# K and Q of the later units read in pieces of two tokens, transposed in two halves by VectorE, in a new order of steps

## The chip, the core and the metric

The kernel runs on one core of one Trainium2 chip. The core has TensorE (matrix products, "PE" in the profile, with its weight loads "PEld"), VectorE ("DVE"), ScalarE ("ACT"), GpSimd ("POOL") and SyncE ("SP"), which run beside each other and meet by semaphores, and 16 DMA engines between HBM and on-chip memory. The metric is the time of one execution in microseconds.

## The reference

A layer of linear attention with the delta rule, and on its output a mixer with a low-rank token product and a two-layer channel network. Batch 4, 8 heads, 768 tokens, 48 values a head, all in 32-bit floats; the mixer has 384 channels, 1536 hidden ones and rank 32.

```python
k_n = k / (np.linalg.norm(k, axis=-1, keepdims=True) + 1e-06)
for t in range(S):
    y[:, :, t] = np.einsum('bhd,bhde->bhe', q[:, :, t], state)
    v_old = np.einsum('bhde,bhd->bhe', state, kt)
    state = state + bt[:, :, :, None] * np.einsum('bhd,bhe->bhde', kt, vt - v_old)
...
x = attn_out.transpose(0, 2, 1, 3).reshape(B, S, H * D)
h = x.transpose(0, 2, 1) @ U @ V
u = x + h.transpose(0, 2, 1)
out = u + np.maximum(u @ w_ch1, 0.0) @ w_ch2
```

## The kernel before

**Units and chunks.** A batch element has two units (`NU = 2`) of 384 tokens; a unit is all 8 heads over 6 chunks (`UC`) of 64 tokens (`L`). There are 8 units `n`; unit `n` lives in `slots[n % 2]`, 9792 floats on each of 128 partitions, in which `views` cuts overlapping places: `kn` and `qn` (K and Q, tokens on partitions), `kq` (K and Q transposed, values on partitions), `pg` and `qk` (products K K' and Q K'), `diag` (the 32x32 diagonal blocks of K K', which share their place with `qk`), `vn` (V).

**A unit's work.** `load` (L311) fetches K, Q and V, on the queue of SP for heads 0 to 3 and of GpSimd for heads 4 to 7 (K of unit 0 partly on ScalarE's). `grams` (L407) brings K and Q into `kq` and forms their products (`products`, L444, matmuls L451); ScalarE copies the diagonal blocks into `diag` (L456 and L460 from unit 3 on, L463 with VectorE's L466 before) and the whole product into `pg` (L470); VectorE masks the products with Q (L478). `blocks` (L491) transposes the diagonal blocks into `gs` (L511), inverts them by substitution on VectorE (L520, L522), transposes back (L526, L533), and joins the blocks to chunks on TensorE (L581 to L634, with copies L643 and memsets L647). `recur` (L655) then walks the chunks in order: prediction from the state (L729, or L753 in the first two units), its difference from V (L735, L760), correction (L742, copied by L745), state update (L770, added by L776), and the outputs (L677, L684), copied to `X` by L667.

**How K and Q reach `kq`.** In units 0 and 1 TensorE transposes them (L231). From unit 2 on (`n >= NU`), K is loaded a second time, as `kb`, and Q only so, in blocks of 32 tokens: partitions are the 32 tokens, one block after another lies along the row, values 0 to 31 on one quarter of the partitions and 32 to 47 on the next (L331 to L335). `turn_blocks` (L433) waits for them and lets VectorE transpose 32x32 blocks straight into `kq`, one instruction of 768 elements a partition for each pair `j` of head groups (L440). K's blocks lie in the place of `pg`, Q's in that of `qn`.

**The mixer.** `front` (L979, L1105, L1108) does the token product, `wide` the channels: first product L1182 with ReLU L1152, second product L1270 added to `X` by L1216 and stored by L1225; L1007 is the first product of the first tokens, done ahead. Six columns of the hidden layer are summed cross-wise (L1203, L1210), so that seven products of half size do for eight. The last batch element uses another scheme of products (L960, L945, L930, L941). Some steps exist in two forms: on the whole 128x128 array, or cut into four 64x64 parts (`crossed`, L219) so that they share a tiling with the recurrence; a "q" in the order chooses the second.

**What sets the order.** The parts are generators; each yields before every step the engine it is for, and `run` (L191 on) resumes them in the sequence of `ORDER`, a list of some 2,700 numbers, each the number of a part, with a bank of the accumulators after a dot. So `ORDER` is the program order of all engines and of both DMA queues at once. `need` makes a part wait until others have emitted a key; it only orders the program, and semaphores between the engines follow from what each instruction reads and writes.

Of the kernel before, what the change touches and what calls it, by code (L numbers as in the profile page):

```python
# [14 lines left out]
L = 64  # L15
BK = 32
# [7 lines left out]
def kernel(ctx: ExitStack, tc: tile.TileContext, q: bass.AP, k: bass.AP, v: bass.AP, beta: bass.AP, moe_U: bass.AP, moe_V: bass.AP, moe_w_ch1: bass.AP, moe_w_ch2: bass.AP, out: bass.AP):  # L24
    nc = tc.nc
# [9 lines left out]
    UC = NC // 2  # L35
# [47 lines left out]
    295 71 295 294 71 61 294 61 294 61 71 297 179.1 294 61 75 300 298 295.2 68 71 295 298 301q 295 294 300  # L83
# [6 lines left out]
    162 330 311 9 329 328 328 328 328 328 329.1 333 329 331 325.0 329 9.2 334q 329 9 334 9.1 325 334 9 9.2  # L90
    334 9 325 334 345.1 9.2 346 9 9.2 345 335q 9 345 61 345 9.2 335 9 347.1 325 9.2 335 335 9 348.0 335 9.2
    347 349 9 9.2 347 336q 9 330 330 336 347 348 9.2 89 89 89 89 205 205 205 205 205 205 205 205 90 90 90 90
# [3 lines left out]
    362 341q 359 362 359 362 341 359 359 85 360.2 357 341 341 357 352 78 357 78 78 9.0 341 78 9 9.1 360 364  # L96
    9 360 363 360 9.0 78 365.1 78 85 9 9.2 342q 9 85 85 85 85 9.0 78 342 9 85 85 365 85 366.2 342 9.0 85 365
# [3 lines left out]
    371 107 85 106 85 344 180 107 106 106 85 107 85 85 180.2 85 372 180 181.0 85 372 97 92 373q 333 350 87  # L101
# [6 lines left out]
    387 102 102 102 383 391 407 391 407 10 102 102 406.1 10.0 102 182q.2 10 102 408 10.0 102 408 182 409 102  # L108
    102 102 409 10 102 102 102 10.2 420 406 405.0 10 406 102 10.2 410q 102 10 102 405 410 406 102 405 421.2
    102 10.1 410 410 10 10.0 410 10 422.1 102 421 423 10.0 102 10 102 421 10.0 421 411q 10 10.2 422 411 10  # L110
# [153 lines left out]

    def blocked(n, i):
        return slots[n % 2][:, 7680:9216] if i else slots[n % 2][:, 4608:6144]

    def in_blocks(n, i):
        return blocked(n, i).rearrange('p (j g x t) -> p j g x t', j=2, g=2, t=BK)
    units = [views(slots[n % 2]) for n in range(N)]  # L270
# [1087 lines left out]
```

## Time and profile before

| | |
|---|---|
| Median of 3 runs | 582.97 us (580.89 to 583.97) |
| Profiled execution | 582.44 us |
| Its span, first to last instruction | 580.0 us |
| Mean granted TensorE clock | 0.976 |
| TensorE, VectorE, ScalarE, GpSimd busy | 538.4, 406.9, 239.7, 134.0 us |
| DMA | 89194 packets, 35.12 MB |

Busy times are from the profiled execution. An engine that is busy little can still be waited for; the chain that ended last follows from the last instruction back to what released each step. A line of the groups reads: line, engine, operation, what it writes and reads, shapes, count, then total busy us and mean ns, then idle time of that engine just before and what ended it.

### The profile page before, as it was taken

The numbers are of one execution on the slowest core, as the hardware profiler recorded it, in microseconds if no ns is written. First come the engines' busy times: TensorE is split into PE (matmuls) and PEld (weight loads), VectorE is DVE, ScalarE is ACT, GpSimd is POOL, SyncE is SP. The second block draws the span as 40 slices with busy tenths as digits, with TensorE's granted clock in tenths as the row PEclk, the third lists the DMA queues.
The fourth block names the chain that finished last, engine by engine and source line by source line (L and its number), as shares of the span: only waits on it lengthen the run. The fifth ranks groups of instructions, "written<-read, shape, count | busy, mean of one in ns | idle before, by whom it ended". The sixth has DMA issues, their size and how long they took to land.

```text
span 580.0 us, 24828 instructions
## 1 busy us (share of the span) xinstructions
PE 538.4 (93%) x11061; PEld 449.4 (77%) x11061; DVE 406.9 (70%) x1010; ACT 239.7 (41%) x523; POOL 134.0 (23%) x229
## 2 busy tenths in 40 slices
PE   5666788999999999999999999999999999999997
PEld 4555676669779778789879877989889769656997
DVE  5799776899969346999978789987713344656532
ACT  3786775442423545146144532632343330346000
POOL 8141341642200470723018207400010000000000
PEclk9998669999989999999999999999999999999999
DMA  9977654450300252530133223220000100000001
GB/s 144 185 191 189 166 147 97 73 102 16 88 13 2 45 114 29 105 78 19 33 44 75 60 39 73 45 62 3 17 2 3 45 2 1 27 0 1 28 15 41
DMA packets 89194, 35.12 MB, mean 61 GB/s; under 512 B 75200, under 2 KB 86976, under 8 KB 89088
## 3 DMA queue, kind: packets, MB, share of 16 engines
q1 hardware_dynamic: 80800, 24.10, 19.9%
q0 software_dynamic: 6688, 9.15, 7.7%
q8 instruction: 86, 1.41, 1.0%
q10 hardware_dynamic: 1600, 0.30, 0.3%
q14 instruction: 20, 0.16, 0.1%
HBM read 28.80 MB, written 4.72 MB: 58 GB/s over the span
## 4 chain that ended last, share of the span: by engine, by line
PE 82%; DVE 6%; issue 4%; DMA 3%; ACT 2%; SPq 1%; POOL 0%; DVEq 0%; POOLq 0%
PE P L1270 25%; PE P L1182 15%; PE P L219 10%; PE P L960 7%; PE P L451 3%; PE P L1007 2%; PE P L742 2%; PE P L677 2%; PE P L729 2%; PE P L770 2%; PE P L684 2%; DMA slot<-in_k_dram 1%; PE P L1105 1%; PE P L979 1%; DVE xt L522 1%
## 5 line engine op out<-in xcount | busy, mean ns | idle before, releaser
L1182 PE MATMUL P<-ut,w_sb 128*128 128x256 f32 x384 | 91.0, 391 | 0.8 <-issue 0.5
L1182 PEld LDWEIGHTS P<-ut,w_sb 128*128 128x128 f32 x384 | 72.2, 193 | 12.6 <-issue 1.8
L1270 PE MATMUL P<-w_sb,hs 128*128 128x192 f32 x456 | 79.3, 329 | 0.0
L1270 PEld LDWEIGHTS P<-w_sb,hs 128*128 128x128 f32 x456 | 74.1, 190 | 1.7 <-DVE X L1216 0.7
L522 DVE TENSOR_TENSOR xt<-xt,prod 128x112 f32<-128x112 f32 (+21 forms) x200 | 64.1, 320 | 5.2
L520 DVE TENSOR_TENSOR prod<-gs,xt 128x112 f32<-128x112 f32 (+21 forms) x200 | 63.8, 319 | 4.7
L1216 DVE TENSOR_TENSOR X<-X,P 128x192 f32<-128x192 f32 x85 | 29.3, 349 | 51.1 <-PE P L1270 46.9
L1152 ACT ACTIVATE hs<-P 128x512 f32<-128x512 f32 x48 | 28.7, 597 | 73.5 <-PE P L1182 56.2
L219 PE MATMUL P<-ut,w_sb 64*64 64x256 f32 x768 | 51.2, 382 | 0.3
L667 ACT COPY X<-P 64x192 f32<-64x192 f32 x96 | 30.0, 312 | 34.8 <-PE P L684 33.7
L647 POOL MEMSET slot<- 32x384 f32 x32 | 13.7, 431 | 127.5 <-PE P L618 56.0
L1270 PE MATMUL P<-w_sb,S 128*128 128x192 f32 x240 | 41.6, 329 | 0.0
L1270 PEld LDWEIGHTS P<-w_sb,S 128*128 128x128 f32 x240 | 38.9, 190 | 0.8 <-DVE prod L520 0.6
L643 ACT COPY slot<-zz 32x384 f32<-32x384 f32 x64 | 34.4, 542 | 12.1 <-DVE zz L599 6.1
L451 PE MATMUL P<-slot 48*64 48x64 f32 x1536 | 33.4, 241 | 6.3 <-ACT slot L428 4.6
L335 POOL DMA_DIRECT2D slot<-in_k_dram x48 | 30.2, 635 | 37.5 <-issue 29.2
L451 PEld LDWEIGHTS P<-slot 48*64 48x64 f32 x1536 | 30.1, 153 | 10.1 <-ACT slot L428 5.0
L335 POOL DMA_DIRECT2D slot<-in_q_dram x48 | 29.9, 628 | 34.0 <-DVE rest L735 21.5
L776 DVE TENSOR_TENSOR s<-s,P 128x192 f32<-128x192 f32 x40 | 14.0, 350 | 32.1 <-PE P L770 25.6
L342 POOL DMA_DIRECT2D slot<-in_v_dram x32 | 21.1, 664 | 50.2 <-DVE s L776 17.0
L219 PEld LDWEIGHTS P<-ut,w_sb 64*64 64x64 f32 x768 | 25.3, 133 | 8.3 <-ACT seen L224 0.8
L1270 PE MATMUL P<-w_sb,slot 128*128 128x192 f32 x180 | 30.4, 327 | 0.9 <-DVE X L1216 0.9
(188 smaller groups left out, 1005.3 us busy)
## 6 DMA issues: line engine op xcount, KB each, us to landing
w_sb<-in_moe_w_ch_dram SPq DMA_DIRECT2D x14, 384.0 KB, 5.2
out_dram<-X SPq DMA_DIRECT2D x22, 192.0 KB, 2.0
slot<-in_k_dram SPq DMA_DIRECT2D x36, 72.0 KB, 3.9
slot<-in_k_dram POOLq DMA_DIRECT2D x32, 72.0 KB, 3.2
slot<-in_v_dram POOLq DMA_DIRECT2D x32, 72.0 KB, 3.3
slot<-in_v_dram SPq DMA_DIRECT2D x32, 72.0 KB, 3.3
X<-in_moe_w_ch_dram SPq DMA_DIRECT2D x6, 384.0 KB, 4.9
wide<-in_moe_w_ch_dram SPq DMA_DIRECT2D x4, 384.0 KB, 4.7
```

The lines of the kernel that those rows point to most:

```text
L219: nc.tensor.matmul(to[half(g)], w[half(r), half(g)], x[half(r)], start=start, stop=stop, skip_group_check=True)
L335: queue.dma_start(out=in_blocks(n, int(name == 'q'))[quarter(2 * par + y), j, g, :, 0:cols.stop - cols.start], in_=of[:, :, cols])
L451: nc.tensor.matmul(p_g[half(g ^ par * i), par, c], kq[rows, c, j, 0, half(g)], kq[rows, c, j, i, half(g)], start=True, stop=True)
L520: nc.vector.tensor_tensor(out=prod, in0=gb[:, :, j, j + 1:, None].to_broadcast([128, split, w, m]), in1=xb[:, :, j:j + 1, 0:m].to_broadcas ...
L522: nc.vector.tensor_tensor(out=xb[:, :, j + 1:, 0:m], in0=xb[:, :, j + 1:, 0:m], in1=prod, op=ALU.subtract)
L643: nc.scalar.copy(pg[quarter(i), :, at, :, a:a + BK], thirds(h)[quarter(i)].rearrange('p r (c j) t -> p r c j t', j=2))
L667: nc.scalar.copy(x[half(c % 2), c // 2, 4 * D * g:4 * D * (g + 1)].rearrange('p (j r d) -> p r j d', r=2, d=D), states(p_y)[half(g)])
L960: nc.tensor.matmul(banks[x], w1_sb[:, 4 * a[0] + e, a[1]] if isinstance(a, tuple) else w1_mixes[a][:, e], tokens(*t) if isinstance(t, tupl ...
L1152: nc.scalar.activation(hs[:, fs[0]:fs[1] + 1:fs[1] - fs[0]], p_f, ACTF.Relu)
L1182: nc.tensor.matmul(p_f[:, x], w(x, t), ut[:, t], start=t == 0, stop=t == KT - 1)
L1216: nc.vector.tensor_tensor(out=to, in0=to, in1=p, op=ALU.add)
L1270: nc.tensor.matmul(to, of[0], of[1], start=of[2], stop=of[3], skip_group_check=True)
```

## The change

K (`kb`) and Q of units 2 to 7 are read in pieces of two neighbouring tokens, 96 values that are contiguous in memory. Partition `t` gets tokens 2t and 2t+1 of each chunk: on the first quarter values 0 to 79 of the 96, on the next 32 to 95. Token 2t's values start at column 0 of a piece and token 2t+1's at column 48, so VectorE now transposes twice (`u` 0 and 1), each time 32 columns of every piece, and writes every second column of `kq`. Pieces are 80 columns wide in place of 32 columns for each token: K's occupy columns 4608 to 6527 of the slot, which reaches into `diag`, and Q's 7680 to 9599. For this the wait for both of K's transpositions moves ahead of the copies to `diag`. DMAs are as many as before. In the changed program the lines from the end of `ORDER` to L264 stand one higher in number, those from there to `turn_blocks` one lower (L335 becomes L334), L440 and L451 stay, and all later ones stand one higher (L456 becomes L457, L1182 becomes L1183).

`ORDER` is a new list throughout, of 2,694 tokens in place of 2,670; the banks and the sequence of almost all steps differ. Of it only the first line of each list is shown.

```diff
-    0 1 0 150 1 149 0 1 2 0 1 37 37 36 37 36 22 14.0 36 22 36 2 213 213 21 39 2 38 37 15.1 21 39 38 39 214.2
+    0 1 0 149 1 0 1 2 0 1 37 37 36 37 36 2 2 14.0 38 37 36 22 36 213 213 22 21 147 15.1 38 39 38 22 38 214.2
...
@@ -262,11 +263,9 @@
         diag = slot[:, 6144:6144 + BK * BK].rearrange('p (e t r) -> p e t r', t=BK, r=2)
         return (kn, kq, pg, qk, qn, vn, diag, kz)
 
-    def blocked(n, i):
-        return slots[n % 2][:, 7680:9216] if i else slots[n % 2][:, 4608:6144]
-
-    def in_blocks(n, i):
-        return blocked(n, i).rearrange('p (j g x t) -> p j g x t', j=2, g=2, t=BK)
+    def in_pairs(n, i):
+        at = (4608, 7680)[i]
+        return slots[n % 2][:, at:at + 4 * UC * (D + BK)].rearrange('p (j c g w) -> p j c g w', j=2, g=2, w=D + BK)
     units = [views(slots[n % 2]) for n in range(N)]
     nc.vector.memset(P[:, :, 0:256], 0.0)
     for i in range(2):
@@ -328,11 +327,11 @@
             if name == 'kb' or name == 'q' and n >= NU:
                 for s in range(4):
                     j, par = divmod(s, 2)
-                    of = src[b, 4 * g + s, hf * UC * L:(hf + 1) * UC * L, :].rearrange('(x t) d -> t x d', t=BK)
+                    of = src[b, 4 * g + s, hf * UC * L:(hf + 1) * UC * L, :].rearrange('(c t u) d -> t c (u d)', c=UC, u=2)
                     for y in range(2):
-                        cols = slice(BK * y, min(BK * y + BK, D))
+                        cols = slice(BK * y, (D + BK, 2 * D)[y])
                         yield op(e)
-                        queue.dma_start(out=in_blocks(n, int(name == 'q'))[quarter(2 * par + y), j, g, :, 0:cols.stop - cols.start], in_=of[:, :, cols])
+                        queue.dma_start(out=in_pairs(n, int(name == 'q'))[quarter(2 * par + y), j, :, g, 0:cols.stop - cols.start], in_=of[:, :, cols])
                     if s % 2:
                         emitted((name, n, g, j))
                 continue
@@ -435,9 +434,10 @@
             if i == 0 and j == 0:
                 yield op('pool')
                 nc.gpsimd.memset(diag[:, CS // 2:], 0.0)
-            yield op('dve')
-            of = in_blocks(n, i)[:, j].rearrange('p g (c u) t -> p c g (u t)', u=2)
-            nc.vector.transpose(kq[:, :, j, i].rearrange('p c (g t) -> p c g t', g=2), of)
+            for u in range(2):
+                yield op('dve')
+                to = kq[:, :, j, i].rearrange('p c (g t u) -> p c g u t', g=2, u=2)[:, :, :, u]
+                nc.vector.transpose(to, in_pairs(n, i)[:, j, :, :, D * u:D * u + BK])
             emitted(('turned', n, i, j))
             begin(products(j, i))
 
@@ -450,6 +450,7 @@
                     rows = half(par, D)
                     nc.tensor.matmul(p_g[half(g ^ par * i), par, c], kq[rows, c, j, 0, half(g)], kq[rows, c, j, i, half(g)], start=True, stop=True)
             if i == 0:
+                yield need(*[('turned', n, 0, y) for y in range(2) if n >= NU])
                 to = diag[:, 0:CS // 2].rearrange('p (c j) t r -> p r c j t', j=2)[:, :, :, j]
                 if n >= LIGHT:
                     yield op('act')
@@ -465,7 +466,7 @@
                         yield op('dve')
                         nc.vector.scalar_tensor_tensor(out=to[:, r], in0=p_g[:, r, :, BK:L], scalar=even[:, 1:2], in1=to[:, r], op0=ALU.mult, op1=ALU.add)
                 emitted(('diag', n, j))
-                yield need(*[('diag', n, y) for y in range(2) if n == 0], *[('turned', n, 0, y) for y in range(2) if n >= NU])
+                yield need(*[('diag', n, y) for y in range(2) if n == 0])
                 yield op('act')
                 nc.scalar.copy(pg[:, :, :, j], p_g)
                 for y in range(2) if n in SPLIT else ():
```

More of the change, by code (lines that the diff above doesn't have):

```diff
@@ L53 @@
     ORDER = """
[29 rows of a table removed]
-    295 71 295 294 71 61 294 61 294 61 71 297 179.1 294 61 75 300 298 295.2 68 71 295 298 301q 295 294 300
[6 rows of a table removed]
-    162 330 311 9 329 328 328 328 328 328 329.1 333 329 331 325.0 329 9.2 334q 329 9 334 9.1 325 334 9 9.2
-    334 9 325 334 345.1 9.2 346 9 9.2 345 335q 9 345 61 345 9.2 335 9 347.1 325 9.2 335 335 9 348.0 335 9.2
-    347 349 9 9.2 347 336q 9 330 330 336 347 348 9.2 89 89 89 89 205 205 205 205 205 205 205 205 90 90 90 90
[3 rows of a table removed]
-    362 341q 359 362 359 362 341 359 359 85 360.2 357 341 341 357 352 78 357 78 78 9.0 341 78 9 9.1 360 364
@@ L97 @@
-    9 360 363 360 9.0 78 365.1 78 85 9 9.2 342q 9 85 85 85 85 9.0 78 342 9 85 85 365 85 366.2 342 9.0 85 365
[3 rows of a table removed]
-    371 107 85 106 85 344 180 107 106 106 85 107 85 85 180.2 85 372 180 181.0 85 372 97 92 373q 333 350 87
[6 rows of a table removed]
-    387 102 102 102 383 391 407 391 407 10 102 102 406.1 10.0 102 182q.2 10 102 408 10.0 102 408 182 409 102
-    102 102 409 10 102 102 102 10.2 420 406 405.0 10 406 102 10.2 410q 102 10 102 405 410 406 102 405 421.2
-    102 10.1 410 410 10 10.0 410 10 422.1 102 421 423 10.0 102 10 102 421 10.0 421 411q 10 10.2 422 411 10
[7 rows of a table removed]
@@ L118 @@
-    112 10 441.1 112 112 10.2 112 419 10 112 112 119 443 10.2 447 441 119 447 448q 119 441 10 441 119 119
-    10.2 119 448 119 10 443 459.1 10.2 448 448 10 119 119 448 119 10.0 119 459 119 460 444.2 10 119 459 10.0
-    119 459 119 461.1 10 444 10.0 119 449 119 444 119 449 119 119 119 450 119 462 119 10 119 450 119 119 119
-    10.2 463 461 465.0 10 461 119 10.2 461 451q 119 10 464 10.1 119 451 10 10.2 451 466.1 465 10 119 10.2
-    465 451 465 119 10 119 10.0 119 451 10 119 468.2 467 10.0 10 452 119 119 119 466 119 10.0 464 452 10 119
@@ L123 @@
-    466 466 119 119 453 469 119 119 119 453 119 119 464 468 211 140 140 211 211 211 211 211 211 140 140 141
-    139 140 140 138 212 140 212 140 212 211 212 138 141 141 131 112 470 162 212 468 455q 119 468 212 119 471
-    212 183.0 471 212 141 131 141 455 119 141 119 183 141 455 471 183.1 141 119 455 139 183 139 455 132
-    183q.2 119 474 472.0 119 183 119 475.1 119 119 119 184.2 119 475 473 119 475 456 119 119 475 119 119 472
[5 rows of a table removed]
-    504.2 485.1 11 504 504 11.0 184q.2 11 485 11.0 501 492 11 184 136 136 136 492 136 136 136 494 506 507
@@ L133 @@
-    485 507 494 507 508 501 185.0 509 505.2 11.1 11 501 495q 495 185 493 11.1 510.0 495 505 495 11 505 136
-    505 136 11.1 495 136 11 136 11.2 185.1 511 136 136 496 136 11 136 512 136 136 496 136 136 136 136 513
-    497 514 136 136 136 11.2 515 510 136 515 516q 136 510 136 185 136 11 516 136 11.2 510 516 11 516 531 530
-    529 528 527.1 11.0 516 528 11 531.2 129 531 532 11.0 527 531 517q 527 11 527 517 533.2 11.0 517 517 11
-    11.1 517 11 535.0 534 11.1 533 11 518q 11.1 518 11 11.1 535 518 533 518 11 528 535 518 535 11.1 533
@@ L138 @@
-    531.0 536 531 529.2 529 530 537 519 528 528 537 528 519 520 539 520 521 540 521 523 541 529 530 530 530
-    530 523 543 542 11 542 542 537 524 522 544 529.2 545 529 524 529 529 531 531 538.1 546 11.2 525q 11 11.0
-    525 11 11.2 538 525 11 525 538 538 525 11.0 547.2 548 11 549 11.1 549 526q 11 11.0 526 11 11.1 550.0 552
-    547 11 551 11.1 547 552 553q 547 11 162 514 11.2 553 11 11.1 553 553 11 564.2 11.1 553 11 11.1 565 550
-    564 11 554q 564 564 550 554 566.1 11.2 554 550 554 11 11.0 554 11 568.2 567 11.0 566 11 555q 566 566
@@ L143 @@
-    11.0 555 11 568 555 555 568 568 555 186.1 569 570 556q 186 556 186.0 556 556 186 556 570 186.2 571 186
[11 rows of a table removed]
[30 rows of a table added]
+    295.2 295 294 68 298 301q 294 295 290 74 294 301 44 295.2 295 301 301 295 68 297 295 301 68 68 9.1 68 68
[5 rows of a table added]
+    332 311 329 9 332 61 328 328 328 328 328 328 329.0 333 329 331.2 162 331 329 9.1 334q 331 9 329 324.2
+    9.1 334 9 9.0 334 345.1 330 324 9 162 9.0 324 334 324 9 9.2 334 9 9.0 346 345 347.2 9 345 335q 345 9.0
+    335 9 9.1 335 335 9 335 348.0 9.1 349 347 9 347 9.1 347 336q 9 330 336 330 9.2 348 90 89 90 89 89 90 89
[3 rows of a table added]
@@ new lines @@
+    91 339 330 88 9.2 360 357.0 361 356 341q 357 9 361 357 9.2 357 341 357 85 9 362.0 341 9.2 356 341 356 9
+    78 78 9.1 78 341 9 361 9.2 78 363.1 78 365 9 364 9.2 78 362 342q 9 362 85 362 9.2 342 340 85 366.0 9 363
[4 rows of a table added]
+    371.0 100 180 373 100 104 374q 85 85 101 374 181.1 101 108 109 374 98 374 109 108 98 108 109 374 181
[6 rows of a table added]
+    182q.1 10 102 408 406.0 10.2 102 182 408 407 409 102 407 102 10 102 409 102 102 102 405.1 420 10.2 102
+    406 410q 102 406 10 405 102 405 10.2 406 410 102 10 421.1 102 10.0 410 410 10 102 10.2 410 10 102 10.0
@@ new lines @@
+    423 162 421 422.2 10 102 421 10.0 421 411q 10 102 10.1 102 411 10 424.0 102 10.1 411 422 411 10 422 422
[7 rows of a table added]
+    112 419 10 112 112 112 119 119 10.1 447 441 10 447 448q 443 119 443 10.1 448 119 10 459.2 119 10.1 119
+    448 119 441 448 10 441 119 119 10.1 119 448 10 459 119 444.0 461 119 119 10.1 459 119 459 449 119 10 119
+    119 119 449 119 444 444 460.2 462 10.1 119 450 119 119 119 450 119 10 119 119 10.0 119 463 465.1 460 10
+    119 10.0 460 464 451q 460 10 119 10.2 119 451 10 119 10.0 451 466.2 465 10 119 10.0 465 464 451 10 119
@@ new lines @@
+    465 10.0 119 451 10 119 468.1 467 10.0 119 466 10 119 10.0 119 452 10 119 466 119 162 452 119 119 119
+    453 469 119 119 119 453 119 162 119 468 139 141 141 211 212 212 211 212 211 211 212 212 211 141 140 140
+    212 140 212 141 211 470 162 211 212 468 455q 471 466 140 141 471 468 119 183.0 140 141 119 464 211 131
+    131 141 140 119 139 119 455 140 183 139 140 131 183.2 139 455 119 138 455 141 138 183 455 138 119 119
+    138 183q.1 119 119 132 183 184.0 132 472.2 474 471 475.1 119 472 473 119 472 456 119 119 475 119 119 475
[5 rows of a table added]
@@ new lines @@
+    11.2 503 184q.1 11 502 497 11.2 136 490 11 136 136 497 490 501 136 136 492 506 136 184 136 501 501 492
+    507 507 507 508 136 505.2 509 185.0 136 491 493q 11.1 493 11 136 136 11.1 505 493 136 493 505 11 505 136
+    136 510.1 185 11.2 493 11 136 136 11.2 185.0 511 136 512 136 185 494 136 136 136 136 136 494 136 136 513
+    129 495 136 136 136 514 11 514 11.0 515 510 11 515 516q 510 136 510 136 136 516 527.2 11.0 516 516 531
+    11 529 528 11.1 528 516 11 531.0 531 532 11.1 527 11 517q 527 531 527 517 528 533.1 11.0 517 517 11 528
@@ new lines @@
+    11.2 517 11 535.0 534 11.2 533 11 518q 533 11.2 518 11 11.2 535 518 518 11 535 535 533 518 11.2 529.0
+    536 529 531.1 531 528 529 537 519 530 528 11 530 530 519 530 530 530 520 539 531 520 521 540 531 521 523
+    541 542 542 523 537 543 537 542 524 544 529.0 545 529 522 524 529 529 538.2 546 11.1 525q 11 11.0 525 11
+    11.1 538 525 11 525 538 538 525 11.0 547.1 548 11 549 11.2 549 526q 11 11.0 526 11 547 11.2 552 550.0 11
+    551 547 11.2 547 553q 11 11.1 553 11 564.2 11.1 553 553 11 11.1 553 11 550 11.1 565 564 11 564 554q 550
@@ L155 @@
+    550 564 554 11.1 566.0 554 11 554 11.2 554 11 568.1 567 11.2 566 11 555q 566 566 11.2 555 11 568 555 555
+    568 568 555 186.0 569 570 570 556q 186 570 556 186.2 556 556 186 556 186.1 571 186 163 163 187.0 163 557
[11 rows of a table added]
     """
```

139 rows, old and new, of the table ORDER are left out of this document.

## The prediction

> **What bounds the kernel now.** I read the shares of the page first, then the slices, the chain that ended last, busy time by stretch, TensorE's waits, and the timeline where the recurrence and the mixer alternate.
>
> ```profile
> span 580.0 us, 24828 instructions
> PE 538.4 (93%) x11061; PEld 449.4 (77%) x11061; DVE 406.9 (70%) x1010; ACT 239.7 (41%) x523; POOL 134.0 (23%) x229
> PEclk9998669999989999999999999999999999999999
> PE 82%; DVE 6%; issue 4%; DMA 3%; ACT 2%; SPq 1%; POOL 0%; DVEq 0%; POOLq 0%
> ```
>
> TensorE is busy 538.4 of 580.0 us and holds 82% of the chain. The kernel can shorten only where TensorE does less or idles less; it idles 41.6 us. The stretches tell where (columns: length, then busy us and count of PE, PEld, DVE, ACT, POOL, then granted clock, DMA share, GB/s):
>
> ```profile
> 0.00:87.00 87.00, 59.16 (x1873) 53.05 (x1874) 68.64 (x194) 59.72 (x114) 34.89 (x62) 0.86 0.79 170
> 87.00:116.00 29.00, 26.67 (x791) 19.53 (x793) 20.92 (x43) 15.64 (x32) 11.92 (x21) 1.00 0.46 85
> 116.00:580.00 464.00, 452.55 (x8415) 376.83 (x8404) 317.39 (x774) 164.38 (x378) 87.19 (x148) 1.00 0.18 38
> ...
> 232.00:261.00 29.00, 28.65 (x484) 22.77 (x476) 27.41 (x68) 9.30 (x19) 14.05 (x23) 1.00 0.45 92
> 348.00:377.00 29.00, 29.00 (x651) 24.06 (x649) 27.32 (x69) 13.29 (x28) 16.52 (x28) 1.00 0.30 59
> 551.00:580.00 29.00, 25.15 (x154) 24.55 (x152) 9.80 (x22) 0.00 (x0) 0.00 (x0) 0.99 0.08 28
> ```
>
> TensorE idles 27.8 us of the first 87, where the first two units and the weights are loaded and converted; their loads are cut as before. From 87 to 116 us it idles 2.3, afterwards 11.5, of which 3.9 in the last row, mostly behind the final products. In the rows from 232 and 348, where later units are loaded and prepared, it is busy 28.65 and 29.00 of 29.00 us: there is no DMA wait to remove there, for all the small packets.
>
> **The pieces themselves: DMA.** Each head's 384 tokens of K or Q were read as 384 runs of 128 bytes and 384 of 64; they are now 192 runs of 320 bytes and 192 of 256. The number of DMAs stays (192), runs halve, bytes grow from 72 KB to 108 KB a head. What a packet costs can be bounded from two stretches of hardware queue 1, 225 to 245 us and the first 30 us (packets, MB, share of 16 engines):
>
> ```profile
> q1 hardware_dynamic: 5336, 0.82, 24.3%
> ...
> q1 hardware_dynamic: 8152, 3.21, 68.4%
> ```
>
> The first is 77.8 us of engine time (24.3% of 16 times 20 us), 14.6 ns a packet of 154 bytes; the second 328 us, 40 ns a packet of 394 bytes, in a crowd. A line through both gives some 26 to 31 ns for the new packets and 8 to 12 for the old, so a pair of tokens costs about 56 ns where four packets cost about 41: from nothing to a third dearer for the engines. At a share of 0.45 that is at worst 0.6, still not full. [...]
>
> The landing times, in the page's issue table, and GpSimd's own cost of issuing:
>
> ```profile
> slot<-in_k_dram POOLq DMA_DIRECT2D x24, 48.0 KB, 2.8
> slot<-in_k_dram POOLq DMA_DIRECT2D x24, 24.0 KB, 2.5
> slot<-in_k_dram POOLq DMA_DIRECT2D x32, 72.0 KB, 3.2
> ...
> L335 POOL DMA_DIRECT2D slot<-in_k_dram x48 | 30.2, 635 | 37.5 <-issue 29.2 <-ACT z L745 8.3
> ```
>
> A new piece of 60 or 48 KB should land between 2.5 and 3.2 us after issue, as now. GpSimd's 96 issues take 60 us; with half the runs they may take between 30 and 60. GpSimd is busy 23%, so this is worth 0 on the path. I take 0 for all of the DMA, with 1 us either way: the place where loads in pieces stand in the chain,
>
> ```profile
> 95.61 2.30 DMA slot<-in_q_dram
> ...
> 108.85 2.43 DMA slot<-in_q_dram
> ```
>
> (start, us), lies between 87 and 116 us, where TensorE idles those 2.3 us only.
>
> **The pieces: VectorE.** 24 transpositions of 768 elements a partition become 48 of 384 with writes two elements apart.
>
> ```profile
> L440 DVE STREAM_TRANSPOSE slot<-slot 128x768 f32<-128x768 f32 x24 | 23.0, 966 | 0.3
> L533 DVE STREAM_TRANSPOSE zz<-zz 128x384 f32<-128x384 f32 x22 | 11.8, 562 | 0.6
> L526 DVE STREAM_TRANSPOSE zz<-xt 128x1024 f32<-128x1024 f32 x8 | 10.0, 1245 | 0.2
> ```
>
> Two of 384 cost 1.12 us against 0.97: 0.16 us more, 24 times, 3.8 us. The third row already writes strided, and lies on the line of the other two (0.16 us and 1.05 ns an element give 1.24 us), so the stride costs nothing. VectorE grows to about 411 us. What covers it is the mixer's matmuls: from 232 to 261 us VectorE is 95% busy and TensorE still idles only 0.35 us. I cost it at 0; with the cover gone it is 3.8 us.
>
> **The added wait.** K's pieces now reach over the place of the diagonal blocks, so the copies of those (L456, L460, L463 on ScalarE) wait for both of K's transpositions; until now only the copy behind them (L470) did. In ScalarE's new order L470 stands behind the same copies, as before; nothing overtakes. Behind the waiting copy queue ScalarE's next steps; VectorE's L511, which opens the substitution, waits for it. At most the delay is one more pair of transpositions, 1.12 us, for each of 6 units. The chain gives VectorE 6% in all and TensorE has the mixer's products to go on with: 0 on the path, up to 6.7 us if every one showed.
>
> **The order.** Both programs issue the same matmuls, the same number of each shape, and take the same number of mixer steps, 25, in the form cut into quarters of the array. What differs is how often TensorE changes between the whole array and its smaller tilings: counted in its instruction order, 174 runs of one tiling before, 162 after. A change has a price:
>
> ```profile
> 208.69 0.45 PE L677 MATMUL P<-s,slot 48*64 48x48 f32 x16
> 208.95 0.41 PE L742 MATMUL P<-rest,slot 64*64 64x48 f32 x16
> 209.30 1.56 PE L1182 MATMUL P<-ut,w_sb 128*128 128x256 f32 x6
> 210.79 0.40 PE L770 MATMUL P<-z,slot 64*48 64x48 f32 x16
> ...
> 212.88 0.41 PE L677 MATMUL P<-s,slot 48*64 48x48 f32 x16
> 213.11 0.41 PE L684 MATMUL P<-z,slot 64*64 64x48 f32 x16
> ...
> 216.72 2.86 PE L1182 MATMUL P<-ut,w_sb 128*128 128x256 f32 x12
> 219.51 0.45 PE L742 MATMUL P<-rest,slot 64*64 64x48 f32 x16
> ```
>
> Start to start, 12 whole-array products take 2.79 us and 6 take 1.49, so 6 cost 1.30 and leaving the tiling 0.19. L742 to L1182 is 0.35 where L677 to L684 is 0.23: entering costs about 0.1. That is 0.29 for a round trip, 0.145 a change; 12 fewer save 1.7 us, between 1.2 (0.10 each) and 3.5 (0.29 each).
>
> Second, the recurrence's links (prediction, correction, state, prediction again) each pass through another engine and back. Where too little other work stands between, TensorE waits:
>
> ```profile
> PE P L742 <- DVE rest L735: 1.5, 5, 0.4
> PE P L770 <- ACT z L745: 1.4, 4, 0.5
> PE P L753 <- DVE s L776: 1.0, 3, 0.6
> PE P L729 <- DVE s L776: 0.5, 1, 0.5
> ```
>
> Together 4.4 us. I laid the durations of the rows above on both orders and counted, for each link, the work between its two products. What is missing to 0.55 or 0.6 us (the longest single waits in these rows are 0.4 to 0.6, which I take for a link with nothing between) sums to 6.3 us before, 26 links with under 0.5 us, and 4.6 after, 21 links. Scaled to the 4.4 us seen, that is 1.2 less; it lies between 0 and all 4.4. The early order, by VectorE's work ahead of each milestone, is the same within 2 us, and its changes of load order have no row; I take 0, give or take 2.
>
> **Sum.** Against the profiled execution's 582.44 us (span 580.0 and 2.4 around it; the median of the runs is 582.97): 0 for DMA, 0 for VectorE, 0 for the wait, -1.7 for tilings, -1.2 for links: 579.5 us.
>
> **Rivals.** *The clock takes it back.* A mean clock of 0.86 over the first 87 us is 24 us at half rate, if the rate is either whole or half; single stretches show where:
>
> ```profile
> 55.00:60.00 5.00, 3.34 (x113) 2.61 (x109) 4.90 (x17) 2.10 (x4) 1.51 (x3) 0.50 0.92 269
> 75.00:80.00 5.00, 3.29 (x121) 2.87 (x117) 2.46 (x8) 2.92 (x6) 0.00 (x0) 0.50 0.73 184
> 90.00:95.00 5.00, 3.79 (x163) 3.11 (x154) 0.41 (x2) 3.54 (x5) 0.00 (x0) 1.00 0.87 175
> 160.00:165.00 5.00, 3.68 (x156) 3.00 (x154) 4.68 (x13) 1.63 (x4) 0.00 (x0) 1.00 0.21 29
> 165.00:170.00 5.00, 4.90 (x85) 4.18 (x86) 4.55 (x12) 1.09 (x3) 0.00 (x0) 0.67 0.06 9
> ```
>
> The half rate comes with TensorE two thirds busy, and a short spell follows the row of 160, 3.68 of 5.00 us busy. If the new order waits a little longer at 87 to 116 us (it issues the loads of unit 2 in another order), the halved clock reaches on to where TensorE is the bound: each us of it costs up to 0.5. It outweighs my gain from 5.8 us on; 17 us, some two thirds of the 24 seen, cost 8.5: 588. Against it: the row of 90, 3.79 busy, kept its full clock. [...]
>
> *Nothing comes of it.* VectorE's 3.8 us show wholly, since the substitution of units 3 to 7 keeps it over 90% busy: 583.3, the same. For it: the 95%; against: TensorE's 0.35 us idle.
>
> *More is gained.* The early idle time falls, or that short halved spell goes (1.7 us): with 3 us from both, 576.5, to 573 with the sum's upper bounds.
>
> **Chances and range.** The sum holds: 0.50 (0.41 faster by over 0.5%, that is under 580.1 us; 0.09 within). More is gained: 0.13, faster. Nothing comes of it: 0.14, the same. The clock: 0.23, slower. Half a per cent is about what a measurement of this kernel can tell from no change. Faster 0.54, same 0.23, slower 0.23. The range runs from 573 to 588; the likeliest case alone from 576 to 581.5.
>
> **What would show it.** Right: VectorE busy near 411 us with 48 transpositions of about 560 ns; the four link waits at about 3.2 us; TensorE busy near 536.7; landing times between 2.5 and 3.2 us. Wrong: transpositions well off 560 ns (the stride has a price); TensorE idling in the stretches where VectorE is over 90% busy; a granted clock under 1.00 beyond 85 us; a gain that lies ahead of 87 us, where I claim none.

## The result and the profile after

The changed kernel takes 578.07 us (median of 6 runs, 576.13 to 578.80) against 582.54 for the kernel before in the same rounds: a ratio of 0.9917, 95% interval 0.9888 to 0.9945. Run again unaltered in other rounds, the ratio was 0.9954 (0.9930 to 0.9978). 579.5 us had been predicted. The profiled execution took 578.75 us.

The page after: span, busy times, slices of the granted clock, chain by engine, the two queues that carry the pieces (q1 those that SP issues, q0 GpSimd's), the transpositions and GpSimd's issues.

```profile
span 576.8 us, 24860 instructions
PE 539.2 (93%) x11061; PEld 451.2 (78%) x11061; DVE 406.5 (70%) x1034; ACT 240.0 (42%) x523; POOL 129.1 (22%) x229
PEclk9999769999999999999999999999999999999999
q1 hardware_dynamic: 62368, 25.87, 19.4%
q0 software_dynamic: 6688, 10.92, 8.6%
PE 80%; DVE 7%; DMA 5%; issue 2%; ACT 2%; SPq 1%; POOL 1%; DVEq 0%; ACTq 0%
L440 DVE STREAM_TRANSPOSE slot<-slot 128x384 f32<-128x384 f32 x48 | 25.6, 560 | 12.0 <-PE P L451 5.8 <-DMA slot<-in_q_dram 5.1 <-POOL slot L436 1.0
L334 POOL DMA_DIRECT2D slot<-in_q_dram x48 | 27.6, 580 | 47.0 <-ACT S L550 15.3
```

TensorE is busy 539.2 us (538.4 before) and idles 4 us less. Queue 1 moves 23% fewer packets (80800 before) in nearly the same engine time. The transpositions take 560 ns each, as forecast, but they now wait 12.0 us, 5.8 of it for TensorE; that entry is new. The stretches (columns as in the prediction):

```profile
0.00:87.00 87.00, 62.12 (x1874) 55.81 (x1875) 68.43 (x199) 61.74 (x118) 35.49 (x67) 0.90 0.81 181
87.00:116.00 29.00, 26.39 (x820) 19.70 (x822) 21.01 (x45) 13.93 (x28) 14.25 (x24) 1.00 0.53 115
116.00:576.80 460.80, 450.65 (x8381) 375.70 (x8371) 317.05 (x792) 164.29 (x378) 79.36 (x140) 1.00 0.18 43
145.00:174.00 29.00, 28.54 (x647) 24.38 (x646) 26.84 (x75) 12.16 (x25) 0.85 (x3) 1.00 0.11 29
```

Three of the 4 us of idle time that went lie in the first 87 us, but the work behind them starts hardly earlier for it. Where the profiled gain lies is read best from the starts of the same products in both timelines. The first product of the line L1270 (L1271 after) starts at 128.9 us before and 128.7 after; the 61st at 140.9 and 141.3; the 121st at 181.8 and 178.8; the 841st, near the end, at 570.6 and 567.7. The whole gain of the profiled pair lies between 141 and 182 us. Before, TensorE's timeline has this there (start, us, then in brackets the idle time ahead and its cause):

```profile
161.96 0.99 PE L595 MATMUL P<-zz 32*32 32x16 f32 x96
162.89 0.80 PE L451 MATMUL P<-slot 48*64 48x64 f32 x36
165.10 1.09 PE L451 MATMUL P<-slot 48*64 48x64 f32 x58 [1.42 <-issue]
...
166.40 4.98 PE L1182 MATMUL P<-ut,w_sb 128*128 128x256 f32 x14
```

and after:

```profile
162.53 0.99 PE L596 MATMUL P<-zz 32*32 32x16 f32 x96
163.46 1.63 PE L451 MATMUL P<-slot 48*64 48x64 f32 x96
165.01 4.15 PE L1183 MATMUL P<-ut,w_sb 128*128 128x256 f32 x18
```

The same burst of small products stops for 1.42 us before, in the midst of one line and with nothing to wait for in the data ("issue"), and runs through after. Behind the stop the clock was at half from 166.7 us for 3.4 us: 14 products take 4.98 us where 18 take 4.15. Stop and clock are 1.42 + 1.7 = 3.1 us, the 3 us of the gain. The trace also shows the transfers on the instruction queue, 86 of 16 KB in the span of each; before, one of them starts at 162.87, some 2.2 us ahead of the restart.

### The profile page after: what moved, and what is told of

It reads as the page before. It is cut to its first block, busy times and chain, and to the rows that moved or that the text cites. A ratio compares the mean times of both kernels' runs of the same rounds, so it can differ in the third digit from the quotient of the medians.

```text
span 576.8 us, 24860 instructions
## 1 busy us (share of the span) xinstructions
PE 539.2 (93%) x11061; PEld 451.2 (78%) x11061; DVE 406.5 (70%) x1034; ACT 240.0 (42%) x523; POOL 129.1 (22%) x229
## 3 DMA queue, kind: packets, MB, share of 16 engines
q1 hardware_dynamic: 62368, 25.87, 19.4%
q8 instruction: 86, 1.41, 1.0%
## 4 chain that ended last, share of the span: by engine, by line
PE 80%; DVE 7%; DMA 5%; issue 2%; ACT 2%; SPq 1%; POOL 1%; DVEq 0%; ACTq 0%
PE P L1271 24%; PE P L1183 15%; PE P L220 9%; PE P L961 7%; PE P L451 3%; PE P L1008 3%; DMA w_sb<-in_moe_w_ch_dram 2%; PE P L771 2%; PE P L743 2%; PE P L730 2%; PE P L678 2%; DMA wide<-in_moe_V_dram 2%; PE P L685 1%; DMA slot<-in_k_dram 1%; PE P L1106 1%
## 5 line engine op out<-in xcount | busy, mean ns | idle before, releaser
L1183 PE MATMUL P<-ut,w_sb 128*128 128x256 f32 x384 | 89.1, 385 | 0.2 <-issue 0.2
L1183 PEld LDWEIGHTS P<-ut,w_sb 128*128 128x128 f32 x384 | 71.2, 190 | 11.0 <-issue 1.2
L1271 PE MATMUL P<-w_sb,hs 128*128 128x192 f32 x456 | 79.4, 329 | 0.0
L1271 PEld LDWEIGHTS P<-w_sb,hs 128*128 128x128 f32 x456 | 74.2, 190 | 2.0 <-issue 1.2
L1271 PE MATMUL P<-w_sb,S 128*128 128x192 f32 x240 | 41.6, 329 | 0.5 <-DVE X L1217 0.5
L1271 PEld LDWEIGHTS P<-w_sb,S 128*128 128x128 f32 x240 | 38.9, 190 | 1.1 <-DVE X L1217 0.8
L451 PE MATMUL P<-slot 48*64 48x64 f32 x1536 | 34.6, 244 | 3.9 <-issue 1.7
L334 POOL DMA_DIRECT2D slot<-in_q_dram x48 | 27.6, 580 | 47.0 <-ACT S L550 15.3
L451 PEld LDWEIGHTS P<-slot 48*64 48x64 f32 x1536 | 30.8, 156 | 8.2 <-issue 3.6
L334 POOL DMA_DIRECT2D slot<-in_k_dram x48 | 27.8, 584 | 41.0 <-ACT z L746 36.5
L440 DVE STREAM_TRANSPOSE slot<-slot 128x384 f32<-128x384 f32 x48 | 25.6, 560 | 12.0 <-PE P L451 5.8
L946 DVE TENSOR_TENSOR slot<-slot,P 128x384 f32<-128x384 f32 x36 | 18.8, 551 | 18.5 <-PE P L961 17.1
```

The source lines that it names most:

```text
L334: queue.dma_start(out=in_pairs(n, int(name == 'q'))[quarter(2 * par + y), j, :, g, 0:cols.stop - cols.start], in_=of[:, :, cols])
L451: nc.tensor.matmul(p_g[half(g ^ par * i), par, c], kq[rows, c, j, 0, half(g)], kq[rows, c, j, i, half(g)], start=True, stop=True)
L1183: nc.tensor.matmul(p_f[:, x], w(x, t), ut[:, t], start=t == 0, stop=t == KT - 1)
L1271: nc.tensor.matmul(to, of[0], of[1], start=of[2], stop=of[3], skip_group_check=True)
```

## The experiments

Two theories. *Work in its order*: the new order wins by fewer changes of tiling and shorter links, as predicted. *Places of the fetches*: the page of the kernel before has 86 transfers of 16 KB on the instruction queue (q8, 1.41 MB) for 22122 matmuls and weight loads, about 257 for each; where the border between two such blocks falls in a burst of small products TensorE stops, as for 1.42 us ahead of 165.10 us, and the new order mainly has these borders elsewhere. Beside them stands the price of the pieces. Each ratio is against the kernel before in the same rounds.

**Order and pieces apart.** blocks_new_order has the new order with the old loads, places and single transposition; pieces_old_order has the old order with the pieces and both transpositions in the old one's step, one copy to `diag` of unit 2 later. (Diffs against the changed kernel and the one before.)

```diff
-                    of = src[...].rearrange('(c t u) d -> t c (u d)', c=UC, u=2)
+                    of = src[...].rearrange('(x t) d -> t x d', t=BK)
...
             for u in range(2):
                 yield op('dve')
-                nc.vector.transpose(to, in_pairs(n, i)[:, j, :, :, D * u:D * u + BK])
+                if u:
+                    of = in_blocks(n, i)[:, j].rearrange('p g (c u) t -> p c g (u t)', u=2)
+                    nc.vector.transpose(kq[:, :, j, i].rearrange('p c (g t) -> p c g t', g=2), of)
```

```diff
-            of = in_blocks(n, i)[:, j].rearrange('p g (c u) t -> p c g (u t)', u=2)
-            nc.vector.transpose(kq[:, :, j, i].rearrange('p c (g t) -> p c g t', g=2), of)
+            for u in range(2):
+                to = kq[:, :, j, i].rearrange('p c (g t u) -> p c g u t', g=2, u=2)[:, :, :, u]
+                nc.vector.transpose(to, in_pairs(n, i)[:, j, :, :, D * u:D * u + BK])
```

> The new order of steps, but K and Q of units 2 to 7 loaded in the old blocks of 32 tokens and turned by one VectorE instruction of 768 elements; the wait ahead of the diagonal copies stays. If the order pays (by fewer tilings and shorter links, or by moving the places where TensorE's instructions run out), about 578 us, as the changed kernel. If the pieces pay (fewer packets), about 582 to 583 us, as before.

> The old order of steps with pieces of two tokens and two transpositions at the place of each old one; one diagonal copy of unit 2 moves behind K's second transposition. If the order pays, 582 to 584 us, no better than before; with VectorE's 3.8 us or the added wait exposed, up to 587. If the pieces pay, about 578 us.

> The changed kernel once more, unaltered, as the base for the others on the same chip: 577 to 579 us. Its trace again without a wait over 1 us between 120 and 540 us if stalls have their place in the program, with one at some new place if they fall by chance.

Measured: the new order with blocks 0.9907 (0.9870 to 0.9943); the pieces in the old order 1.0133 (1.0092 to 1.0174); the changed kernel again, beside them, 0.9954, and in its trace no wait of TensorE over 1 us behind 120 us, as expected of stalls that have a place in the program. The new order with blocks is about 1% faster than the kernel before. The pieces cost 1.3% in the old order: 588.75 us, where I had expected 587 at most. In the new order they cost between 0.1 and 0.5%, by overlapping intervals. In the old order VectorE shows where (its timeline, old order with pieces):

```profile
208.63 1.04 DVE L453 STREAM_TRANSPOSE slot<-slot 128x384 f32<-128x384 f32 x2 [1.90 <-DMA slot<-in_q_dram]
209.59 0.52 DVE L1217 TENSOR_TENSOR S<-S,hs 128x384 f32<-128x384 f32 x1
211.51 1.04 DVE L453 STREAM_TRANSPOSE slot<-slot 128x384 f32<-128x384 f32 x2 [1.40 <-DMA slot<-in_q_dram]
212.47 0.32 DVE L790 TENSOR_TENSOR s<-s,P 128x192 f32<-128x192 f32 x1
```

L453 are the transpositions. They wait for pieces of Q that have not landed, the state addition L790 stands behind them, and TensorE behind that:

```profile
PE P L743 <- DVE s L790: 2.0, 1, 2.0
```

From 213.7 us the clock is at half for 3.4 us. Up to 324.71 us L464 (L451) waits 1.6 us for ScalarE's copy to `diag`, and again 3.4 us at half. Together that is 2.0 + 1.6 + 3.4 = 7.0 us, of a loss of 7.7 (1.33% of 580). In the changed kernel neither is there.

**The pieces' price in the new order.** new_two_turns keeps the blocks and only transposes them in two halves; blocks_again repeats the blocks beside it.

```diff
+                of = in_blocks(n, i)[:, j].rearrange('p g (c u) t -> p c g u t', u=2)[:, :, :, u]
+                to = kq[:, :, j, i].rearrange('p c (g u t) -> p c g u t', g=2, u=2)[:, :, :, u]
+                nc.vector.transpose(to, of)
```

> The new order with the old blocks and their loads, but VectorE transposes each block row in two halves of 384 elements, as with the pieces: 48 transpositions of about 560 ns in place of 24 of 966, VectorE 3.8 us busier, nothing else. Theory 1 (the mixer's matmuls cover VectorE): the same as the blocks beside it within 0.3%. Theory 2 (VectorE's extra 3.8 us are the pieces' price): 0.3 to 0.7% above the blocks, with waits of L452 for the transposition of about 1 us. Theory 3 (the pieces' price is DMA and memory): as theory 1 here, so that the half per cent has to lie in the loads.

> The new order with the old blocks, unaltered, as the base for the three kernels beside it. If the ratio of 0.9907 measured for it is a property of the program, it comes out between 0.987 and 0.995 again, and TensorE's waits for 'issue' stand at the same products as before (the one ahead of L772 at about 62 us with some 2.4 us, none over 0.6 us behind it). If its lead over the changed kernel was one chip's or one run's luck, it lies within 0.3% of 0.9954 or above.

Measured: 0.9905 (0.9877 to 0.9933) and 0.9900 (0.9862 to 0.9938). The blocks' ratio came again, though not its stalls as expected: the one at 64.5 us has others of 1.5 and 1.0 us behind it, at 74.4 and 94.0. The second transposition costs nothing that can be measured (0.05%, with intervals of 0.3 to 0.4% either way), and no matmul waits for it: theory 1, or 3, but not 2. VectorE is only 0.8 us busier for it (406.2 against 405.4), not 3.8. What the pieces do cost stands in VectorE's and TensorE's waits (us in total, times, longest), first the changed kernel:

```profile
DVE slot L440 <- PE P L451: 5.8, 5, 2.4
DVE slot L440 <- DMA slot<-in_q_dram: 5.1, 2, 3.4
...
PE P L451 <- DVE slot L440: 0.9, 1, 0.9
```

then the blocks in two turns:

```profile
DVE slot L441 <- DMA slot<-in_q_dram: 6.0, 2, 5.0
DVE slot L441 <- DMA slot<-in_k_dram: 1.2, 1, 1.2
```

With pieces, a transposition waits for products of L451, five times; one of these products then waits 0.9 us for the transposition. With as many transpositions of the same length in the same order, but written 32 columns side by side and not every second one, neither wait is there. The changed kernel's repetition has the same rows (5.7 and 0.9), its 0.9 at the same place, 316 us. Whether the data need the wait, or only the program's way of comparing interleaved regions, was not tried. Nor was the other difference between the two kernels, the pieces' larger place.

**The places of the fetches.** Idle products on TensorE ahead of its first, while it waits for data, move all that follow in its stream of instructions. In the traces 32 of them are 128 instructions (24988 against the changed kernel's 24860), four a product, so that 64 make 256, by estimate one transfer's 257, and 32 half of it. old_shift32 does it to the kernel before, new_shift32, new_shift16 and new_shift64 to the changed one, blocks_shift32 to the new order with blocks; only the count differs.

```diff
+    for _ in range(32):
+        nc.tensor.matmul(P[0:32, 7, 480:512], ident[0:32, 0:32], ident[0:32, 0:32], start=True, stop=True)
```

> The kernel before, with 32 idle 32x32 products issued on TensorE at the very start, where it waits for the first load for 8 us; everything else as before. They move every later place where TensorE's instructions are fetched by half a fetch (64 products of 4 instructions each). If the profiled gain is a stall of 1.4 us at 163.7 us for instructions that have not come, with the halved clock of 3.4 us behind it (1.7 us), that stall goes or moves: 579 to 580 us, and the clock stays at 1.00 from 145 to 174 us. If tilings and links pay, nothing changes: 582 to 583 us. If the pieces pay, nothing changes either.

> The changed kernel with 32 idle products of 32x32 on TensorE ahead of its first, while it has nothing to do yet. The old order lost 1.7% by the same edit. Theory 1 (the new order wins through where TensorE's instruction fetches fall): the gain is lost, 580 to 592 us, with waits for 'issue' over 0.5 us at other places behind 90 us, among them bursts of small products, and perhaps short spells of halved clock. Theory 2 (the new order wins through fewer changes of tiling and shorter links, as predicted): within 0.5% of the changed kernel, 574 to 581 us, with the links' waits unaltered and no new waits for 'issue'.

> The new order with the old blocks and the same 32 idle products at the start. Theory 1 (the pieces themselves cost about 0.4%, whatever the fetches do): 0.2 to 0.7% under the changed kernel with the 32 products, which runs beside it. Theory 2 (pieces and blocks differ only in which fetch happens to stall): any sign, with a difference of up to 1%, and its own waits for 'issue' at the places of the changed kernel with the 32 products but of other lengths.

> The changed kernel with 64 idle products of 32x32 ahead of TensorE's first, twice the 32 that cost it 2.7%. Between two stalls at the same phase lie 64 products or a multiple. Theory 1 (what costs is where the fetches' boundaries fall in the program): 64 products move them by one whole block, so every boundary falls where it fell without any, and the time comes back to 574 to 581 us, with waits for 'issue' behind 87 us of 1 to 3 us in all. Theory 2 (idle products at the start cost by themselves, by the later start of the loads' work or by the clock): 64 cost as much as 32 or more, 593 us and above.

> The changed kernel with 16 idle products at the start, a quarter of a block. Theory 1: another placement of the boundaries, so another time, anywhere from 572 to 596 us, with waits for 'issue' behind 87 us that go with it: under 2 us in all where the time is within 0.5% of the changed kernel, 5 us or more where it is 590 or above. Theory 2: half of what 32 cost, some 585 us.

| kernel | ratio (interval) | waits for "issue" behind 87 us | clock at half behind 95 us |
|---|---|---|---|
| before | 1 | 3.1 us | 3.4 us |
| changed | 0.9917 (0.9888 to 0.9945) | 2.7 | 0 |
| changed, again | 0.9954 (0.9930 to 0.9978) | 1.6 | 0 |
| changed, 16 idle | 0.9978 (0.9952 to 1.0004) | 5.1 | 0 |
| changed, 32 idle | 1.0224 (1.0193 to 1.0255) | 10.2 | 10.2 |
| changed, 64 idle | 0.9993 (0.9968 to 1.0018) | 0.4 | 0 |
| blocks, new order | 0.9907 (0.9870 to 0.9943) | 0.4 | 0 |
| blocks, new order, again | 0.9900 (0.9862 to 0.9938) | 1.8 | 3.4 |
| blocks in two turns, new order | 0.9905 (0.9877 to 0.9933) | 0.5 | 3.4 |
| blocks, new order, 32 idle | 1.0130 (1.0093 to 1.0167) | 10.7 | 3.4 |
| before, 32 idle | 1.0167 (1.0125 to 1.0209) | 7.8 | 3.4 |
| pieces, old order | 1.0133 (1.0092 to 1.0174) | 3.1 | 6.8 |

(The third column is the sum of TensorE's waits put down to "issue", the fourth is read from the granted clock; both from the profiled execution.) 32 idle products cost every kernel 1.7 to 3.1%. 64 cost the changed one only 0.4 to 0.8% (582.04 us, just over the 574 to 581 of theory 1 and far from the 593 of theory 2), and the profiles show why. Against the changed kernel's second profile, 64 bring the first substitution step (L511) 2.5 us later, and from 128 us to the end the products are late by 2.8 to 3.1 us: behind the start nothing is lost. 32 bring that step 0.2 us earlier, yet the end 18.4 us later. Of these, 8.6 us are more waits for "issue" and some 5.1 us the 10.2 us at half clock; the rest was not followed. The waits of the 32 for "issue" (the four largest rows, with the shift lines stand two higher) lie in small products everywhere:

```profile
PE P L707 <- issue: 3.6, 1, 3.6
PE P L453 <- issue: 2.1, 3, 1.5
PE P L687 <- issue: 1.3, 2, 1.0
PE P L633 <- issue: 1.2, 1, 1.2
```

and with 64 there is one:

```profile
PE P L598 <- issue: 0.4, 1, 0.4
```

The idle products by themselves are ruled out as the cause, for twice as many cost less. The sum of these waits does not give the time, however: 16 idle products came to 580.57 us with 5.1 us of waits, which I had expected only at 590 us and above, and with 32 the changed kernel took 595.18 us, over the 592 of theory 1. With 32 in both, the blocks are 0.9% faster than the pieces, clear of noise and more than the 0.2 to 0.7% of a fixed price. For the old order I had expected 579 to 580 us, the stop at 163 us gone; it went from there, and others came at 96.8, 169.7 and 325.0 us (1.5, 1.8 and 1.2 us).

**The price of a change of tiling.** 42 idle products behind L1271's last whole-array ones, on a quarter of the array or on all of it (the expectations say 84; in the records each is two matmuls, and the loop runs 42 times, so there are 84 changes, not 168).

```diff
+                        if (b, i) == (LAST, NG - 1):
+                            nc.tensor.matmul(P[0:64, 0, 448:512], ident[0:64, 0:64], ident[0:64, 0:64], start=True, stop=True)
```

> The changed kernel with 84 idle products on one 64x64 part of the array, 64 columns each, one behind each whole-array product of L1271 of the last tokens (its output goes to unused columns). Against the kernel beside it, where the same products use the whole array, it adds 168 changes of tiling and nothing else. Theory 1 (a change costs TensorE 0.145 us, as the prediction took): 24 us longer than the kernel beside it (168 x 0.145), some 14 to 49 with the bounds of 0.10 and 0.29. Theory 2 (a change costs nothing of its own; the 0.29 a round trip in the trace was the filling and emptying around short groups): within 5 us of it.

> The changed kernel with the same 84 idle products of 64 columns behind the same products of L1271, all on the whole array. By the rate of L1271's own products (192 columns every 0.16 us start to start, two a product) each adds 0.1 to 0.2 us, so 8 to 17 us over the changed kernel. It is the base for the kernel beside it.

Measured: 597.39 and 588.08 us, 1.0267 (1.0213 to 1.0321) and 1.0105 (1.0062 to 1.0149). On the whole array they cost 1.5 to 1.9% over the changed kernel, 9 to 11 us, as expected. The difference of the two of 9.3 us, over 84 changes, is 0.11 us each; 0.145 gave 12.2 and the bounds 8.4 to 24. TensorE's timeline repeats with a period of 0.78 us on the quarter,

```profile
565.90 0.33 PE L1273 MATMUL P<-ident 64*64 64x64 f32 x2
566.16 0.59 PE L1271 MATMUL P<-w_sb,slot 128*128 128x192 f32 x2
566.68 0.33 PE L1273 MATMUL P<-ident 64*64 64x64 f32 x2
```

and 0.55 us on the whole array,

```profile
561.79 0.33 PE L1273 MATMUL P<-ident 128*128 128x64 f32 x2
561.96 0.54 PE L1271 MATMUL P<-w_sb,slot 128*128 128x192 f32 x2
562.34 0.33 PE L1273 MATMUL P<-ident 128*128 128x64 f32 x2
```

so 0.23 for a round trip.

## Why the prediction was right

The time is right, and the size of the order's effects nearly so; but the gain of this kernel is not the sum that gave it. That 579.5 came so near to 578.07 us is luck in part: a cost taken as nothing ate most of the forecast gain, and a stall that went, which the sum does not have, stood in for it.

**Tilings: right in price.** 0.11 us a change against 0.145: 12 fewer are 1.3 us, not 1.7, if a change between other tilings costs the same, which was not tried. Eight of the twelve lie behind 182 us, 0.9 us. TensorE's busy time does not show it: 536.7 us was the sign, and it is 539.2.

**Links: right, in the new order with blocks.** From 182 us to the end TensorE's waits other than "issue" sum to 4.4 us before and 3.3, 3.4 and 3.3 in the three runs of the new order with blocks: 1.1 less, where 1.2 was forecast over the whole kernel. Over that stretch those three gain 2.6, 2.1 and 1.4 us on the kernel before; 0.9 for tilings and 1.1 for links make 2.0. In the changed kernel the links are as short,

```profile
PE P L743 <- DVE rest L736: 0.8, 3, 0.3
PE P L771 <- ACT z L746: 1.1, 4, 0.5
PE P L754 <- DVE s L777: 1.5, 2, 1.2
```

the four named waits 3.6 us with L730's 0.2, not 3.2, since L754 in the first units rose.

**The wait: the step that failed.** The prediction asked only which copies wait for the transpositions and found 0. What costs is the reverse: the transpositions wait for L451, and L451 for them, 0.9 us on TensorE. With it the sum of the waits behind 182 us is 4.4 again, and the changed kernel gains nothing there on the kernel before (0.9 us in its repetition), where the order with blocks gains 1.4 to 2.6. So in these profiles the pieces take back most of what tilings and links bring.

**The rest: a rival's.** What is left of the profiled gain are the 3 us between 141 and 182 us. "More is gained" named that halved spell and its 1.7 us; the 1.42 us ahead of it I had in view only as TensorE being idler from 160 to 165 us. All five profiled executions in the new order without idle products gain 2.9 to 3.5 us there. The stop in front came again in the old order with pieces (164.71 us, 1.18 us), without the halved clock. By the runs with idle products such a stop is a matter of place, not of work.

**VectorE: covered, and over-priced.** VectorE is busy 406.5 us, not 411. Busy time of the transpositions rose by 2.6 us, not 3.8, since neighbours overlap: four in a row take

```profile
311.01 1.96 DVE L440 STREAM_TRANSPOSE slot<-slot 128x384 f32<-128x384 f32 x4
```

0.49 us each; a mean duration of 560 ns counts the overlap twice. Some 1.6 us more went with the order (405.1 and 405.4 us with blocks, against 406.9); the rest of the difference was not followed. That the second transposition is covered is shown by the two turns, for the 0.8 us by which they made VectorE busier. The stride has no price: 558 ns with side-by-side columns, 560 with every second one.

**DMA: right in the sum, wrong in a packet's price.** The durations of the single packets of queue 1 in the traces have the prices apart. Before, a packet of 64 bytes takes 11.0 ns on average and one of 128 takes 13.6; after, one of 256 takes 20.6 and one of 320 takes 22.9. A pair of tokens costs 49 ns in four packets and 43.5 in two, 12% less. The prediction drew a line through mixed packets and had 41 and 56; worked out again, that line gives 34 and 58. Halved packets are not a halved load: with 18432 fewer packets queue 1 takes 19.4% of the engines' time, against 19.9 before. Queue 0 shows no difference: 8.6%, and 7.9 in the repetition, against 7.7 before and 7.9 to 8.6 with blocks in the new order. The landing of the pieces is at the upper end or above what was forecast:

```profile
slot<-in_q_dram POOLq DMA_DIRECT2D x24, 60.0 KB, 2.9
slot<-in_k_dram SPq DMA_DIRECT2D x24, 60.0 KB, 3.4
slot<-in_q_dram POOLq DMA_DIRECT2D x24, 48.0 KB, 3.4
```

GpSimd's 96 issues take 55 us, not 60. One load of K stands in the chain where the prediction had none, behind GpSimd's issues,

```profile
241.57 3.53 DMA slot<-in_k_dram
```

and so it does in the new order with blocks (235.05 us, 3.19). TensorE idles only 0.06 us for it.

**The clock: it did not take the gain back here.** In the changed kernel no halved clock lies between 83 us and the last few, in both profiles; with 32 idle products the rival is real (10.2 us at half, 3% slower than without them).

**Not settled.** The profiled executions of one kernel differ early: the new order with blocks reaches L1270's first product at 125.1 us in one and 133.6 in the other. No gain or loss ahead of 130 us is read from single profiles here. And the new order with the old blocks, 0.9907 and 0.9900, lies below the changed kernel's 0.9917 and 0.9954, but the intervals overlap: the better version is likely, not shown.

## What to carry to other kernels

When an order of steps is changed, a gain of 1% can be the place where TensorE happens to stop for "issue": here 32 idle products at the start cost 1.7 to 3.1%, and 64 cost the changed kernel 0.4 to 0.8%. Move the whole program with idle products, by half the distance of the stops and by all of it, before the order gets the credit. Price an edit of data layout by who must wait for whom on the shared tile, in both directions, and not only by the durations of the instructions. The order, with its places, was worth -1%, and the layout between +0.1 and +1.3%, by the program around it; only apart could that be seen.

## What the runs showed of the hardware

TensorE stops with nothing in the data to wait for. Most waits for "issue" of over 0.5 us lie in bursts of small products and keep a phase: between two of them lie multiples of 64 products, with a slow drift. In the kernel before, the number of TensorE's matmul records (two a product) up to a stop, modulo 128, runs from 88 at 26.9 us to 72 at 165.1; with 32 idle products, these counted in, it runs from 89 to 53 at 467.1. So the stops stay where they are in the stream while the program moves against them: in the changed kernel the waits for "issue" behind 87 us are 1.6 to 2.7 us, with 32 idle products 10.2 and the span 16 to 18 us longer, with 64 only 0.4. The trace has 86 transfers of 16 KB on the instruction queue for 22122 matmuls and weight loads, about 257 each, or 64 products of four. In the kernel before, TensorE goes on after its five waits for "issue" of over 1 us (at 54.38, 60.50, 68.05, 92.77 and 165.10 us) 2.2 to 2.8 us after one of these transfers starts. That the stops wait for them the trace suggests but does not name. One stop took 3.65 us, and the waits for "issue" behind 87 us reached 10.7 (blocks, new order, 32 idle). Behind the stop of 1.42 us the clock was at half for 3.4 us; behind the one of 1.18 us in the old order with pieces it was not. Two of these transpositions in a row on VectorE overlap by some 0.07 us (0.49 us each in a row of four, 0.56 by their own durations). A change between the whole array and a quarter cost 0.11 us, with 64x64 products between 128x128 ones.
